# Loading queries by rows of a block and turning them by transposing transfers in half of the batches of a fused attention and Fourier-MLP kernel

## The chip, the core and the metric

The kernel runs on one core of one Trainium2 chip. A core has five engines that run side by side, each with its own queue: PE (TensorE, the matrix unit, whose loads of weights are listed as PEld), DVE (VectorE), ACT (ScalarE), POOL (GpSimd) and SP (SyncE, which here only issues transfers). Transfers issued by SP, ACT or POOL run on 16 DMA engines; those that POOL issues can change the type on the way (here float32 in HBM to float16 in SBUF). The metric is the device time of one execution in microseconds. The profile is one execution, recorded by the hardware profiler.

## The reference

Shapes: four batches, eight heads, 768 tokens in eight blocks of 96, head size 64, model width 512, hidden width 2048.

```python
P = sort_net                                   # (4, 8, 8, 8)
for _ in range(5):                             # softmax of rows, then columns scaled to 1
    P = exp(P - max(P, -1)); P = P / sum(P, -1); P = P / sum(P, -2)
k_sorted = einsum('bhij,bhjcd->bhicd', P, k_b) # blocks of k and v mixed by P
v_sorted = einsum('bhij,bhjcd->bhicd', P, v_b)
scores = q_b @ k_sorted.T / 8                  # within each block of 96 only
attn = softmax(scores)
x = attn @ v_sorted                            # -> (4, 768, 512)

u = x + real(fft(fft(x, axis=1), axis=2))
un = (u - mean(u)) / sqrt(var(u) + 1e-6)
out = u + relu(un @ w_ch1) @ w_ch2
```

## The kernel before

**Stages.** For each batch there are five stages. The mixing makes `kz` (the sorted keys, channels on partitions) and `vs` (the sorted values) by matmuls with `kron`, a spread-out form of the sort matrix. The queries are turned so that channels lie on partitions (`qT`). The attention goes over four pairs of heads `hp`, each in two halves `y` of four blocks. The Fourier stage makes both transforms from folded sums and differences by matmuls with constant cosines and sines. The MLP runs over two groups of three tiles of tokens: 64 matmuls of 384 columns (line 1180), a relu, and 48 matmuls of 512 columns (line 1198), then the output is added and stored. Weights lie in SBUF for the whole run. The main program goes through the batches and hands out the steps of batch b's attention, of batch b+1's loads and mixing, of batch b's Fourier stage and its MLP.

**The order.** Nothing is issued at once. Each piece of work is a step with a name, a batch, the engines that could do it and an assumed duration, the buffers it reads and writes, and, for transfers, an assumed time on the DMA engines (`work`, `hop`). At the end `Plan.run` simulates the engines and puts out one step after the other, the one with the earliest start and among near ones the one with the best priority. Priorities and release times come from tables with an entry for each step's name and batch (`LEAD`), for single steps (`MOVE`) and for loads (`REL`, in nanoseconds). So every engine's queue has a fixed order, written by this planner. `fill` puts dummy matmuls (`unread`, line 687) into planned gaps of PE as long as the plan's clock is below `FILL_END`. Before a load that is marked `bulk=2`, `before` picks an earlier load that has to have landed first, and POOL waits for it with a copy of one element (line 493); POOL's later work queues behind that.

**Buffers** are taken from rings: three each for a pair's keys and queries (`k16`, `q16`), six for its values (`v16`), four for turned queries (`qT`), three for exponentials (`es`, `eT`).

**Loads.** A pair of heads of q, k or v is one transfer by POOL's queue (lines 559 and 569). Partition p takes six tokens that follow each other in HBM, 6p to 6p + 5, so one piece in HBM is 6 x 64 float32 values, 1536 bytes, and a load has 128 x 2 pieces.

**Queries.** `q_mix` turns a pair by 12 transposes on PE through the identity into one bank of PSUM (line 800), and one copy by ACT or DVE writes `qT` (lines 547 and 551). Because of the load, tokens within a block come out as `PERM`: place 16 g + c holds token 6 c + g. That order goes through the attention and is undone by the constants of the Fourier stage and by the selection matrix `rsel`, which are built with `PERM`. In batches 1 to 3 the transposes of a pair are one step with that pair's key matmuls (`psQK`); in batch 0 they are steps of their own (`psQ`).

**Attention.** In batches 0 and 1 (`4 * b + hp < TURN`) `maxima` and `scores` compute the products twice, the second time with keys on partitions, so that the exponentials need no turning. In batches 2 and 3 `turned` computes them once, with queries on partitions; the exponentials are turned by transposing transfers on SP's queue (step `turn_e`, line 912), two for each half. SP's queue also has the transposes of normalised rows (`turn_u`, line 1153, batches 1 to 3) and the moves of sorted values from `vo` to `vs` (line 783).

Of the kernel before, what the change touches and what calls it, by code (L numbers as in the profile page):

```python
# [10 lines left out]
F16 = mybir.dt.float16  # L11
# [6 lines left out]
S = 768  # L18
D = 64
NB = 8  # L20
BLK = 96
KM = BLK + 24
G = 6
# [4 lines left out]
SCALE = 0.125  # L28
TURN = 8
# [5 lines left out]
PERM = np.array([6 * (p % 16) + p // 16 for p in range(BLK)])  # L35
# [172 lines left out]
class Plan:  # L208
# [5 lines left out]
    FILL_LOW, FILL_END, WINDOW = 1931, 49895, 3413  # L214
    LAG, PE_TAIL, MARGIN, NEAR = 45.0, 250.0, 120.0, 14.0
    PORT, PORT_WAIT = ("fold", "fold_d", "minus", "nm", "un", "xem", "kron"), 450.0
    OVER = {"V": 80, "A": 100}
    SPARE = 909
    REL = dict(cdh=38223, cse=17364, cso=12887, idx=43588, load_k2=82421, load_k3=45767, load_q1=32871,
        load_q2=83959, load_q3=155044, load_v1=26759, load_v2=99397, load_v3=18886, rsel=30643, w0=38071,  # L220
        w1=51566, w2=7303, w3=34666, w4=62534, w5=56660, w6=23527, w7=18919)
    LEAD = dict(P=(-10.9, -33.1, 10.8, 47.7), Q=(-21.5, 0, 0, -19.8), We=(-1.6, -0.2, 0.2, 0),
        Wo=(24.9, -10.8, 0, -20.3), a16=(-11.2, -16.6, 1.4, 0), a_out=(26.9, 10.9, 36.1, -20.1),
        add=(-68, 0, 74.6, -10.9), amr=(0.9, 2.6, 18, 0), amt=(-58.6, -2.5, -4.5, 0), const=(15.9, 0, 0, 0),
        exp=(10.9, 48.2, 35.7, -8.7), fold=(-27.1, -23.4, -64.4, 3.7), fold_d=(0, -4.8, 34.7, 0.1),
        hold=(-53, 0, 0, 0), kron=(2.5, 74.7, 2.1, 37.8), kz=(-20.2, 0.8, -52.6, -46.3),
        load_k16=(0, 75.7, 0, -47.8), load_q16=(0, 7.8, -23.1, -0.3), load_v=(0, 26.7, -51.4, -35.5),
        m8=(6.6, 0, 0, 0), max=(-79.4, -48, -32.6, -52.3), minus=(-40.1, -17.1, -9.6, -5.8),
        nm=(-1, -10.8, -13.3, 71.6), norm=(4.5, -39, -29.1, -35.3), ot=(43.5, 40.4, -18.7, 0),
        outt=(0, 0, -51.4, -37), patch=(3.2, 28.2, 5.1, -43.2), pc=(9.3, 0, 0, 0), pca=(19.5, 0, 0, 0),  # L230
        pcol=(-10, 0, 0, 0), pcs=(28.9, 0, 0, 0), ph=(83.6, 26, 3.3, -1.1), psA=(0, 2.4, 0, -26.9),
        psB=(7.1, 0, 2, 26.3), psF=(5.8, -0.3, 0, 19.8), psG=(71.5, 0, 0, 0), psK=(-31.8, 17.3, 37.2, 0.7),
        psM=(-45.2, 0, 0, 0), psN=(-18, -17.6, 7.4, 67), psP=(20.4, 0, 0, 0), psQ=(53.7, -3.6, 23.4, -2.4),
        psQK=(0, 8, 17.6, -16.7), psR=(-1.8, 58.2, 0, 1.6), psRh=(32.2, 16.3, 7.5, -22.1),
        psS=(47.1, 34.2, -65.3, -27.4), psT=(-29.9, -33.5, 0, 0), psV=(-64.4, 0, 24.7, -4.5),
        psWe=(-51.6, 33.5, 1.3, 0), psWo=(4.8, 37.8, 2.9, 0), psX=(26.8, 14.2, -8.8, 0), psY=(0, 25.5, 0, 0),
        psaT=(-0, -2.4, 10.7, 0.2), ptm=(-12.5, 0, 0, 0), qT=(-5.1, 0, 5.8, -57.3), relu=(1.5, 0, 9.6, 81.6),
        root=(0, 9.5, 9.1, -21.3), row_zero=(0, -26.2, -15.6, -2), stats=(-6.4, -23.2, -10.4, 1.7),
        store=(-1.5, 0, -29.6, 6.6), turn_e=(0, 0, 0, -18.6), turn_u=(0, 0, 26.1, 10.7),
        u=(37.5, 8.6, 31.2, -14.6), un=(48.6, 33.2, -20.3, -21.5), unT=(0, 62.4, 0, 15.1),  # L240
        v_move=(-23, 23.6, 0, 26.2), v_sum=(0, -10.6, 0.2, 43), vg=(65.5, 0, 0, 0),
        vo=(14.8, -41.4, -78.1, 0), weights=(62.6, 0, 0, 0), xem=(-20.9, -4.2, 0, -9),
        xom=(-38.7, 63.9, 0, 1.4))
    MOVE = dict(P={(1, 2): 15.5}, add={(2, 2): 0.8, (2, 4): 65.3, (3, 2): 44.7, (3, 4): 9.4},
        amt={(3, 0): -11.9}, const={(0, 3): -19.1},
# [1188 lines left out]
```

## Time and profile before

| | |
|---|---|
| median of 3 runs | 292.35 us (292.27 to 296.48) |
| the profiled execution | 291.53 us, of which 289.7 us lie between its first and last instruction (its span) |
| mean granted clock of PE in it | 0.985 |
| DMA queue q0 (issued by POOL) | 19040 packets, 19.40 MB, 40.6% of 16 engines' span |
| DMA queue q1 (issued by SP) | 31574 packets, 10.28 MB, 18.9% |
| loads of q and of k | 16 each, 192 KB as written |
| transposing transfers | 32 of exponentials, 18 of normalised rows |

A group's row gives the line, the engine, the operation, what it writes and reads, and the count; then the busy time in all and the mean of one in ns; then the idle time of the engine just before such instructions, and what ended it. A row of the timeline gives start and duration in us, the engine, the line and the count, with the idle time before it in brackets. A row of a stretch gives the busy time of each engine in it, with the number of instructions, then the granted clock (1.00 is full), the mean share of the 16 DMA engines' time and GB/s. Matmuls overlap in the array, so the mean of one is its passage and not its share of PE's time; the difference of two starts is.

### The profile page before, as it was taken

The numbers are of one execution on the slowest core, as the hardware profiler recorded it, in microseconds if no ns is written. First come the engines' busy times: TensorE is split into PE (matmuls) and PEld (weight loads), VectorE is DVE, ScalarE is ACT, GpSimd is POOL, SyncE is SP. The second block draws the span as 40 slices with busy tenths as digits, with TensorE's granted clock in tenths as the row PEclk, the third lists the DMA queues.
The fourth block names the chain that finished last, engine by engine and source line by source line (L and its number), as shares of the span: only waits on it lengthen the run. The fifth ranks groups of instructions, "written<-read, shape, count | busy, mean of one in ns | idle before, by whom it ended". The sixth has DMA issues, their size and how long they took to land.

```text
span 289.7 us, 6877 instructions
## 1 busy us (share of the span) xinstructions
PE 276.1 (95%) x2598; PEld 161.9 (56%) x2598; DVE 191.5 (66%) x435; ACT 183.8 (63%) x455; POOL 122.0 (42%) x190
## 2 busy tenths in 40 slices
PE   7899999689999999999999999999999999999993
PEld 2467766257765565445555576455645645645541
DVE  6749988978797897673679998987866572001011
ACT  2368976778894779746495679788725832712700
POOL 8473736314226789765833256230023641112010
PEclk9979999979999999999999999999999999999998
DMA  7998969998856876969935862553311025002002
GB/s 101 182 162 169 154 106 163 185 140 136 107 88 104 112 147 96 124 143 186 130 88 113 154 112 38 115 144 75 70 38 38 36 54 129 36 34 77 1 36 74
DMA packets 50847, 30.41 MB, mean 105 GB/s; under 512 B 25962, under 2 KB 48900, under 8 KB 50812
## 3 DMA queue, kind: packets, MB, share of 16 engines
q0 software_dynamic: 19040, 19.40, 40.6%
q1 hardware_dynamic: 31574, 10.28, 18.9%
q8 instruction: 20, 0.33, 0.5%
q10 hardware_dynamic: 200, 0.30, 0.4%
q14 instruction: 13, 0.11, 0.2%
HBM read 28.50 MB, written 6.29 MB: 120 GB/s over the span
## 4 chain that ended last, share of the span: by engine, by line
PE 78%; DVE 14%; DMA 3%; issue 2%; ACT 1%; DVEq 0%
PE bank L1180 29%; PE bank L1198 24%; PE bank L983 3%; PE bank L853 3%; PE bank L937 3%; DMA eT<-es 2%; PE bank L1088 2%; PE bank L875 2%; PE bank L821 2%; PE bank L761 2%; PE bank L1005 1%; PE bank L800 1%; DVE st L1115 1%; PE bank L1045 1%; DVE mxs L863 1%
## 5 line engine op out<-in xcount | busy, mean ns | idle before, releaser
L1198 PE MATMUL bank<-w2sb,hr 128*128 128x512 f16 x384 | 90.0, 379 | 0.0
L1180 PE MATMUL bank<-unT,w1sb 128*128 128x384 f16 x512 | 89.2, 329 | 0.0
L1186 ACT ACTIVATE hr<-bank 128x384 f16<-128x384 f32 x128 | 60.7, 495 | 38.7 <-PE bank L1180 37.9
L1180 PEld LDWEIGHTS <-w1sb 128*128 128x128 f16 x512 | 49.1, 99 | 32.2 <-issue 1.5
L1219 POOL DMA_INDIRECT out_dram<-outt,idx_sb x22 | 22.6, 1026 | 88.5 <-DVE outt L1207 70.0
L1198 PEld LDWEIGHTS <-hr 128*128 128x128 f16 x384 | 36.0, 98 | 38.2
L1207 DVE SCALAR_TENSOR_TENSOR outt<-u,bank 128x512 f32<-128x512 f32 x24 | 16.4, 682 | 41.8 <-PE bank L1198 41.8
L892 ACT ACTIVATE sm<-bank,mns 96x96 f32<-96x96 f32 x128 | 32.3, 352 | 2.4 <-DVE mns L898 2.0
L944 DVE TENSOR_TENSOR xr<-bank,rz 96x512 f16<-96x512 f32 x32 | 22.0, 686 | 1.1
L547 ACT CAST W<-bank 128x384 f16<-128x384 f32 (+1 forms) x38 | 12.8, 380 | 12.9 <-PE bank L983 8.5
L1115 DVE BATCH_NORM_STATS2 st<-u 128x6 f32<-128x512 f32 x24 | 16.4, 681 | 4.0 <-POOL u L1101 3.9
L863 DVE TENSOR_REDUCE mxs<-bank 96x8 f16<-96x768 f32 x16 | 14.5, 949 | 5.6 <-PE bank L853 5.5
L1100 POOL TENSOR_TENSOR u<-u,PQ 128x257 f32<-128x257 f32 x18 | 12.8, 711 | 9.9 <-DVE PQ L1058 8.6
L898 DVE TENSOR_REDUCE mns<-bank 96x8 f32<-96x768 f32 x16 | 15.0, 944 | 2.6 <-PE bank L853 2.2
L1101 POOL TENSOR_TENSOR u<-u,PQ 128x255 f32<-128x255 f32 x18 | 12.6, 699 | 3.6 <-DVE PQ L1058 3.6
L908 ACT ACTIVATE es<-sm 96x384 f16<-96x384 f32 x19 | 10.0, 528 | 6.1 <-DMA eT<-es 5.8
L880 ACT ACTIVATE sm<-bank 96x768 f32<-96x768 f32 x16 | 12.8, 801 | 1.4 <-PE bank L853 1.2
L922 ACT ACTIVATE eT<-sm 96x768 f16<-96x768 f32 x16 | 13.4, 841 | 0.4
L569 POOL DMA_DIRECT2D k<-in_k_dram x15 | 11.0, 733 | 5.9 <-PE bank L821 4.8
L937 PEld LDWEIGHTS <-eT 97*128 97x128 f16 (+1 forms) x256 | 11.2, 101 | 3.8 <-ACT eT L922 0.5
L943 DVE RECIPROCAL rz<-bank 96x8 f32<-96x8 f32 x32 | 6.3, 197 | 10.6 <-PE bank L937 10.5
L983 PE MATMUL bank<-cso_sb,xso 120*128 120x384 f16 (+1 forms) x64 | 13.1, 326 | 0.0
(144 smaller groups left out, 426.5 us busy)
## 6 DMA issues: line engine op xcount, KB each, us to landing
vs<-vo SPq DMA_DIRECT2D x48, 65.0 KB
v<-in_v_dram POOLq DMA_DIRECT2D x16, 192.0 KB, 4.9
k<-in_k_dram POOLq DMA_DIRECT2D x15, 192.0 KB, 5.5
q<-in_q_dram POOLq DMA_DIRECT2D x15, 192.0 KB, 4.1
w1sb<-in_moe_w_ch_dram POOLq DMA_DIRECT2D x4, 512.0 KB, 8.0
w2sb<-in_moe_w_ch_dram POOLq DMA_DIRECT2D x4, 512.0 KB, 5.9
eT<-es SPq DMA_TRANSPOSE x32
cdh_sb<-cdh SPq DMA_DIRECT2D x1, 387.0 KB
```

The lines of the kernel that those rows point to most:

```text
L863: ("max", b, {"V": 945}, lambda e: nc.vector.tensor_reduce(mxs[n].t.rearrange("p (t j) -> p t j", t=2), pair(pS, BLK), axis=AX.X, op=ALU.max),
L892: nc.scalar.activation(sm.t[:, i], pair(pS, BLK)[:, t, i % 4], AF.Exp, bias=mn.t[:, i:i + 1], scale=-1.0)
L898: ("max", b, {"V": 945}, lambda e: nc.vector.tensor_reduce(mn.t.rearrange("p (t j) -> p t j", t=2), pair(pS, BLK), axis=AX.X, op=ALU.min), ...
L937: nc.tensor.matmul(ps[0:wide(i).stop - BLK * i, i // 4, i % 4], et[0:97, wide(i)], vs[b % 2][:, 4 * y + i % 4, (D + 1) * h:(D + 1) * (h + 1)])
L944: nc.vector.tensor_tensor(xr2[b % 2][0:BLK, 4 * y:4 * y + 4, 128 * hp:128 * hp + 128].rearrange("p j (t d) -> p t j d", t=2), ps[:, :, :, ...
L983: nc.tensor.matmul(ps, x[0:n, j], cso[0:n, j, :], start=(j == 0), stop=(j == 3))
L1115: nc.vector.bn_stats(st.t, us[b, i, m].t)
L1180: nc.tensor.matmul(ps, w1sb[:, mc, 128 * fc:128 * fc + 128], unT[b, gr].t[:, mc, :], start=(mc == 0), stop=(mc == 3))
L1186: nc.scalar.activation(dst, bank(pH, [128, 384]), AF.Relu)
L1198: nc.tensor.matmul(ps, hr[f4].t[:, fc % 4, 128 * t:128 * (t + 1)], w2sb[:, fc, :], start=(fc == 0), stop=(fc == 15))
L1207: step("outt", b, {"V": 687}, lambda e, u=u, pC=pC, o=o: nc.vector.scalar_tensor_tensor(o.t, u.t, RSC, bank(pC, [128, DM]), op0=ALU.mult, ...
L1219: step("store", b, {"G": 1050}, lambda e: nc.gpsimd.indirect_dma_start(out=out.rearrange("b s m -> (b s) m"), out_offset=bass.IndirectOffs ...
```

## The change

- All loads of q get a partition for each row in natural order. In batches 0 and 1, partition p takes tokens 128 g + p for g = 0 to 5 (one transfer, pieces of 64 values, 256 bytes). In batches 2 and 3, partition r of 96 takes row r of each of the eight blocks, in two transfers, one for each head of the pair.
- `PERM` becomes the identity; the copies that write `qT` in batches 0 and 1 become contiguous.
- In batches 2 and 3 the transposes on PE and the copy go. A new step `turn_q`, two for each pair, turns four blocks at a time by a transposing transfer on SP's queue, from `q16` straight into `qT`. The key matmuls of these batches are steps of their own (`psK`).
- A `q16` buffer is 128 x 1024 float16 values in place of 128 x 768; `v16` has five buffers in place of six.
- `TURN` counts batches in place of pairs; which batches use `turned` stays as it was.
- The planner's tables are new throughout, as are some of its settings: `FILL_LOW` 1931 to 1834, `FILL_END` 49895 to 81377, `NEAR` 14 to 68, `SPARE` 909 to 1392, and the release times, among them `load_q1` 32871 to 17265, `load_q2` 83959 to 49545, `load_v3` 18886 to 94052.

```diff
-TURN = 8
+QT = 2
+TURN = 2
...
-PERM = np.array([6 * (p % 16) + p // 16 for p in range(BLK)])
+PERM = np.arange(BLK)
...
-    ring("q16", 3, [128, 2, G * D], F16)
-    ring("v16", 6, [128, 2, G, D], F16)
+    ring("q16", 3, [128, NB, 128], F16)
+    ring("v16", 5, [128, 2, G, D], F16)
...
+    def flat(t, x, by_row):
+        if by_row:
+            return rows(t).rearrange("p h (g d) -> p (h g) d", d=D), x.rearrange("h (g p) d -> p (h g) d", g=G)
+        return t, x.rearrange("h (p g) d -> p h (g d)", g=G)
...
+            if b >= QT and tag == "q16":
+                step("load_q16", b, {"G": 1700}, lambda e, t=d[b, hp]: [nc.gpsimd.dma_start(
+                    t.t[0:BLK, :, D * hh:D * hh + D],
+                    q[b, hs.start + hh].rearrange("(i r) d -> r i d", r=BLK)) for hh in range(2)],
+                    w=[d[b, hp]], work=3000, hop=1750, lanes=2, bulk=2 if b > 1 else 1, need=need, rel=f"load_q{b}")
+                continue
...
-                t.t, src[b, hs].rearrange("h (p g) d -> p h (g d)", g=G)),
-                w=[d[b, hp]], work=1250, hop=1750, bulk=2 if b > 1 else 1, need=need, rel=f"load_{tag[0]}{b}")
+                *flat(t.t, src[b, hs], src is q)),
+                w=[d[b, hp]], work=1250 if tag == "k16" else 1700, hop=1750, bulk=2 if b > 1 else 1, need=need, rel=f"load_{tag[0]}{b}")
...
-            copy(e, qT[b, hp].t.rearrange("x (i g c) -> x i g c", g=G, c=16),
-                 bank(pQ, [128, G, 128], F16).rearrange("x g (i c) -> x i g c", c=16))
+            copy(e, qT[b, hp].t, bank(pQ, [128, S], F16))
+        if b >= QT:
+            for t in range(2):
+                step("turn_q", b, {"S": 1300}, lambda e, t=t: nc.sync.dma_start(
+                    qT[b, hp].t[:, 384 * t:384 * t + 384].rearrange("x (i r) -> x i r", r=BLK),
+                    q16[b, hp].t[0:BLK, 4 * t:4 * t + 4].rearrange("q i x -> q (i x)"), transpose=True),
+                    r=[q16[b, hp]], w=[(qT[b, hp], t)], work=800, hop=900)
+            return
...
+        if b >= QT:
+            q_mix(b, hp)
         mixed = ("kz", b, {"A": 790, "V": 950}, ev, [pK], [("kz", hp)])
-        if b == 0:
+        if b == 0 or b >= QT:
             plan.chain(("psK", b, {"T": 350}, f, [k16[b, hp], (kron[b], hp)], [pK]), mixed)
             return
```

More of the change, by code (lines that the diff above doesn't have):

```diff
@@ L222 @@
[L222 to L243, printed above, removed]
@@ L244 @@
[L244 to L253 removed]
+    SPARE = 1392
@@ L562, in load_v, with rows @@
             w=[v16[b, hp]], work=1200, hop=1800, bulk=2 if b > 1 else 1, need=need, rel=f"load_v{b}")
+    def flat(t, x, by_row):
+        if by_row:
+            return rows(t).rearrange("p h (g d) -> p (h g) d", d=D), x.rearrange("h (g p) d -> p (h g) d", g=G)
+        return t, x.rearrange("h (p g) d -> p h (g d)", g=G)
+    def rows(t):
+        return t if t.shape[1] == 2 else t.rearrange("p i x -> p (i x)")[:, 0:2 * G * D].rearrange(
+            "p (h x) -> p h x", h=2)
     def load_kq(b, hp, need, q_first=False):
```

80 lines of the change are left out of this document (59 added, 21 removed).

## The prediction, written before the changed kernel was run

> **What bounds the kernel now.** I read the head of the page first, then the chain that ended last, then a table of stages that I cut where the work changes: at 12.3 us the softmax iterations on the sort matrix end, at 60.5 us the first matmul of batch 0's MLP starts, at 221.8 us only the last of batch 2's MLP is left beside the end of batch 3's attention, and at 243.7 us batch 3's own MLP starts.
>
> ```profile
> span 289.7 us, 6877 instructions
> PE 276.1 (95%) x2598; PEld 161.9 (56%) x2598; DVE 191.5 (66%) x435; ACT 183.8 (63%) x455; POOL 122.0 (42%) x190
> ...
> PE 78%; DVE 14%; DMA 3%; issue 2%; ACT 1%; DVEq 0%
> ```
>
> ```profile
> 12.30:60.50 48.20, 42.72 (x627) 28.95 (x627) 39.77 (x92) 36.44 (x66) 24.95 (x35) 0.95 0.96 154
> 60.50:100.00 39.50, 39.50 (x500) 25.45 (x499) 31.21 (x67) 30.42 (x65) 15.35 (x28) 0.97 0.77 116
> 100.00:160.00 60.00, 58.98 (x512) 33.73 (x511) 43.90 (x89) 42.07 (x123) 39.22 (x67) 1.00 0.81 129
> 160.00:221.80 61.80, 61.74 (x554) 35.41 (x553) 51.45 (x112) 44.85 (x136) 17.11 (x24) 1.00 0.43 91
> 221.80:243.70 21.90, 21.90 (x134) 12.11 (x133) 12.00 (x28) 10.69 (x26) 11.23 (x15) 1.00 0.22 55
> 243.70:285.30 41.60, 41.51 (x224) 21.73 (x222) 4.13 (x6) 15.57 (x32) 4.84 (x5) 1.00 0.16 48
> ```
>
> In each row stand the stretch, its length, the busy time of PE, PEld, DVE, ACT and POOL, the granted clock, the DMA share and GB/s. There are two regimes. Up to 60.5 us PE leaves 5.48 us of 48.2 idle, DVE is busy for 39.8 us and the DMA engines are taken for 96% of the time: this stage is set by DVE and by transfers. From 60.5 to 285.3 us PE is idle for 0.00 + 1.02 + 0.06 + 0.00 + 0.09 = 1.2 us in all, at a clock of 0.97 to 1.00. There the MLP of one batch fills PE under the attention of the next, so what leaves PE's queue shortens the run one for one, as long as the other engines keep up.
>
> **The transposes that leave PE.** For batches 2 and 3 each of the eight pairs of heads loses 12 transposes through the identity (line 800). Two pairs of the last batch and one of batch 2 in PE's timeline, with the group's row:
>
> ```profile
> 116.49 0.53 PE L800 MATMUL bank<-ident,q 128*64 128x128 f16 x12
> 116.85 0.50 PE L821 MATMUL bank<-kron,k 128*64 128x128 f16 x12
> ...
> 167.12 0.53 PE L800 MATMUL bank<-ident,q 128*64 128x128 f16 x12
> 167.47 0.50 PE L821 MATMUL bank<-kron,k 128*64 128x128 f16 x12
> 168.04 0.53 PE L800 MATMUL bank<-ident,q 128*64 128x128 f16 x12
> 168.37 0.53 PE L821 MATMUL bank<-kron,k 128*64 128x128 f16 x12
> ```
>
> ```profile
> L800 PE MATMUL bank<-ident,q 128*64 128x128 f16 x180 | 8.1, 228 | 0.5 <-DMA q<-in_q_dram 0.4
> ```
>
> The 228 ns of one is its passage and overlaps with its neighbours. What counts is from start to start of the next group: 0.36, 0.35 and 0.33 us. I take 0.35 us, and 8 x 0.35 = **2.8 us** leave the queue in the stretch where PE is full. The k matmuls behind them stay, so no turn between array shapes is saved. The Trainium skill ("TensorE: Matmul & The Clock Gate", "Part 4: PE-mode transpose") has about 275 ns for one such transpose in a kernel; 96 of them would then be an estimated 26 us, and the trace, with 12 in 0.35 us, does not agree.
>
> **The evictions that leave with them.** Between 84 and 200 us the queries were moved out of PSUM like this:
>
> ```profile
> L551 DVE COPY qT<-bank x6: 540/543/558, 93.5 to 181.3; 128x768 f16<-128x768 f16 x6
> L547 ACT COPY qT<-bank x2: 793/822/852, 117.4 to 168.7; 128x768 f16<-128x768 f16 x2
> ```
>
> That frees 6 x 0.54 = 3.3 us of DVE and 2 x 0.82 = 1.6 us of ACT. I cost it at nothing: in those stages the end is PE's, and DVE has 16 of 60 and 10 of 61.8 us to spare. At the most it takes away part of PE's 1.2 us of waits. In batches 0 and 1 the copies stay, only their target becomes contiguous; their rows are those of a copy of 768 elements and I leave them as they are.
>
> **The order and the fill.** All lead times of the planner change, and dummy matmuls may now go into PE's gaps up to 81.4 us instead of 49.9. Between 50 and 60 us PE idles, and the first MLP matmuls behind that run slowly:
>
> ```profile
> 50.00:60.00 10.00, 6.13 (x59) 3.69 (x58) 9.61 (x29) 7.02 (x16) 4.04 (x7) 0.96 1.06 161
> ```
>
> ```profile
> 60.49 2.47 PE L1180 MATMUL bank<-unT,w1sb 128*128 128x384 f16 x8
> 62.80 0.61 PE L1162 MATMUL bank<-ident,un 128*128 128x128 f16 x8
> ...
> 67.67 1.47 PE L1180 MATMUL bank<-unT,w1sb 128*128 128x384 f16 x8
> 68.98 0.51 PE L875 MATMUL bank<-small_sb,mxs 96*128 96x96 f16 x8
> ```
>
> The same eight matmuls take 2.31 us to the next start at 60.5 and 1.31 us at 67.7. Dummies in the gap can win back at most that 1.0 us; they win nothing if planned idle and real idle do not meet. A dummy that meets work delays it by a fraction of a microsecond. I take the middle, **0.5 us**. What the other lead times do, no row can say; it is in the rivals.
>
> **The loads of q.** All 16 now read pieces of 256 B: 128 x 12 (batches 0 and 1) or 2 x 96 x 8 (batches 2 and 3), 1536 pieces in either form, where there were 256 of 1536 B. The trace has no such load. Nearest rows, by stretches in which one kind of packet prevails: from 2 to 12 us (loads of 1536 B), 48 to 58 us (with weight rows of 2 KB), 129 to 140 us (mostly moves of v, 520 B) and 193 to 209 us (transposing transfers, 256 B).
>
> ```profile
> q0 software_dynamic: 1926, 1.40, 105.0%
> ```
>
> ```profile
> q0 software_dynamic: 1897, 1.71, 115.3%
> ```
>
> ```profile
> q1 hardware_dynamic: 1630, 0.74, 29.7%
> ```
>
> ```profile
> q1 hardware_dynamic: 4672, 1.11, 34.9%
> ```
>
> The share times 16 engines times the stretch, over the packets, gives 87, 97, 32 and 19.1 ns for one. So a load takes 256 x 87 / 16 = 1.4 us of all engines today. At 19.1 ns the new one takes 1536 x 19.1 / 16 = 1.8 us, 0.44 us more; at 87 ns it would take 8.4, 7.0 us more. I take 19.1 ns, since the piece is of that size and one engine's time for a packet should grow with its bytes; both ends stay for the range. A gain is excluded, as the bytes are the same. The eight loads of batches 0 and 1 then cost 3.5 us of DMA time ahead of the weights. What covers it:
>
> ```profile
> 40.78 0.72 POOL L569 DMA_DIRECT2D q<-in_q_dram x1 [4.35 <-PE bank L800]
> ...
> 82.81 0.29 POOL L493 COPY landed<-w2sb 1x1 f16<-1x1 f16 x1 [7.51 <-DMA w2sb<-in_moe_w_ch_dram]
> ```
>
> ```profile
> 63.99 0.53 PE L800 MATMUL bank<-ident,q 128*64 128x128 f16 x12
> ...
> 88.61 1.03 PE L1198 MATMUL bank<-w2sb,hr 128*128 128x512 f16 x4
> ```
>
> Batch 1's last query load is issued at 40.8 us, and the first of that batch's queries are turned only at 64.0. The last part of w2 has landed at 82.8 and is first used at 88.6: 5.8 us of cover, more than 3.5. So this costs **0** at 19.1 ns, and the excess over 5.8 us beyond it. Batch 2 and 3 loads have 19% and 57% of the DMA time free (stages above). The Trainium skill ("DMA: Bandwidth & Descriptors", "Specifications") wants at least 512 B for full rate and says that smaller pieces are written by read-modify-write, which speaks against this load; no row here shows it for a load.
>
> **POOL and the buffer of v.** Eight loads are issued in two halves, and each issue writes more pieces:
>
> ```profile
> L569 POOL DMA_DIRECT2D q<-in_q_dram x15 | 11.0, 732 | 5.0 <-PE bank L800 4.3 <-issue 0.5
> L1236 POOL DMA_DIRECT2D w2sb<-in_moe_w_ch_dram x4 | 3.1, 771 | 0.5 <-issue 0.5
> ```
>
> From 256 to 512 pieces an issue grows by about 40 ns, so 768 pieces should take some 0.8 us: 8 more issues are about 6 us of POOL, plus the waits of later loads for earlier ones to land. Behind them queue the sums of v, the additions to u and the stores; POOL is idle for 21 us between 100 and 160 and for 45 us of the next stage, and I cost it at nothing. Without that cover each half would delay an addition by 0.8 us. One v buffer fewer holds a load back until one more reader is done:
>
> ```profile
> 137.44 0.74 POOL L559 DMA_DIRECT2D v<-in_v_dram x1 [0.88 <-PE bank L1180]
> ```
>
> Such a wait exists, of 0.9 us, and is hidden. Zero again.
>
> **SP's queue.** Sixteen transposing transfers are added, of the shape of those that turn the exponentials.
>
> ```profile
> L912 SPq DMA_TRANSPOSE eT<-es x32: 1180/1200/2384, 98.3 to 208.3; - x32
> ```
>
> ```profile
> 177.16 3.16 SPq L1153 DMA_TRANSPOSE unT<-un x2
> ...
> 192.99 16.50 SPq L912 DMA_TRANSPOSE eT<-es x11
> ```
>
> ```profile
> 238.81 0.81 ACT L1138 ACTIVATE un<-u,nm,rstd 128x512 f16<-128x512 f32 x1 [2.44 <-DMA unT<-un]
> ...
> 243.52 2.76 PE L1180 MATMUL bank<-unT,w1sb 128*128 128x384 f16 x16
> ```
>
> At 1.2 us each they are 9.6 us of SP for a batch. Behind them on SP stand the turns of the exponentials, the moves of v and the turns of the normalised rows, and PE's values and MLP wait for those. From 177.2 to 209.5 us SP's queue is full; a turn of q put in there pushes all that by 1.2 us. The end of that chain is batch 3's third normalised tile: its transfer has landed by 238.8, when its buffer is taken again, and PE starts that MLP at 243.5. So there are 4.7 us of slack, of which a run shorter by 3.3 us uses most. If the turns of q come before 177 us the cost is 0, which I take.
>
> **The sum.** The profiled execution took 291.53 us, 1.8 more than its span. 291.5 - 2.8 - 0.5 = 288.2. The median of the runs shown, 292.35, lies 0.8 above that execution, so the forecast for a median is **289.0 us**, 1.1% less.
>
> **Rivals.** *The pieces of q choke the early DMA.* At 32 ns a load costs 1536 x 32 / 16 - 1.4 = 1.7 us more, eight cost 13.4, and 13.4 - 5.8 = 7.6 us show: 289.0 + 7.6 = 296.6. Between 87 and 97 ns lie 512 B, so a line through these two puts 256 B at some 62 ns: 8 x (5.95 - 1.4) - 5.8 = 30.6, about 320 us. It decides from 22 ns on, where eight loads use up the 5.8 us. For it speaks that only the rows of q0 are reads from HBM with a cast; against it, that packets there overlap (105%) and so look longer than they are, and that batch 0's MLP is not the only work PE has. This is also the way in which the 512 B rule of the Trainium skill's DMA page would act. Chance 0.20; half of it above 298.
> *SP's queue takes the gain.* Four turns of q within the full stretch push the chain by 4.8 us; with the slack of 4.7 and PE earlier by 3.3, 3.4 us show, and the time is 289.0 + 3.4 = 292.4, no change. For it speaks that the last query copy of batch 3 started at 181.3 us, inside that stretch; against, that batch 2's last queries leave their buffer at 116.9 us, so that batch 3's can be loaded and turned long before 177 us. Chance 0.15.
> *The new order also empties the early stage.* PE's 5.5 us of idle before 60.5 us and the clock behind it are worth up to 6.5 us; half of it, instead of my 0.5, gives 286.2, all of it 283.0. For it: every lead time there is new. Against: DVE, at 39.8 of 48.2 us, loses no work there. Chance 0.25.
> *The forecast itself*: 0.40.
>
> **Chances and range.** Two per cent, about what a measurement of this kernel can tell from no change, is 5.8 us: below 286.5 or above 298.2. Faster: four fifths of the third rival and little else, 0.21. Slower: half of the first rival, 0.10, and 0.01 for mishaps. Within: 0.68. The range runs from 284.5, the middle of the third rival, to 296.5, the first rival at 32 ns.
>
> **What would show it.** In the new profile line 800 has 96 matmuls fewer, PE is still full from about 60 us on, and the last MLP starts some 3 us earlier. Query loads that land in more than about 6 us, or PE waiting for w2 or k before 90 us, mean the first rival; a PE gap before the last MLP, with SP full ahead of it, the second; PE idle before 60 us well under 5.5 us, the third. If PE idles by more than 3 us after 60 us, the step that what leaves PE leaves the run was wrong.

## The result and the profile after

| | before | after |
|---|---|---|
| median | 293.26 us (292.27 to 296.48, 4 runs) | 302.41 us (300.36 to 302.99, 4 runs) |
| ratio of the times, 95% interval | 1 | 1.0355 [1.0304, 1.0406] |
| profiled execution, span | 291.53 us, 289.7 us | 302.81 us, 299.8 us |
| first MLP matmul, last one with `w1sb`, begin at | 60.5 us, 274.5 us | 66.5 us, 284.6 us |

A ratio counts only executions within 1.5% of the fastest of their kernel, so it is not the quotient of these medians. The change makes the kernel slower by 3.0 to 4.1%. The forecast was 289.0 us, 1.1% faster, with a range that ended at 296.5. The head of the page of the changed kernel, its queue of POOL's transfers, and the chain that ended last:

```profile
span 299.8 us, 6731 instructions
PE 278.2 (93%) x2513; PEld 159.2 (53%) x2513; DVE 188.5 (63%) x430; ACT 183.7 (61%) x452; POOL 133.4 (45%) x198
...
q0 software_dynamic: 39648, 19.40, 47.2%
...
PE 64%; DVE 16%; DMA 9%; ACT 4%; issue 3%; POOL 2%; SPq 0%; DVEq 0%; POOLq 0%; ACTq 0%
```

PE has 85 matmuls fewer and is busy for 2.1 us more; its idle time grew from 13.6 us (289.7 - 276.1) to 21.6. Its share of the chain fell from 78% to 64%, and DMA, ACT and POOL came in. The same stages as before (columns as there), of the changed kernel:

```profile
12.30:60.50 48.20, 40.76 (x623) 27.75 (x623) 38.78 (x82) 32.51 (x57) 28.05 (x37) 1.00 1.21 166
60.50:100.00 39.50, 37.15 (x476) 23.41 (x475) 30.55 (x70) 31.31 (x61) 12.13 (x21) 1.00 0.74 97
100.00:160.00 60.00, 58.29 (x479) 31.70 (x472) 39.20 (x78) 38.02 (x114) 44.47 (x73) 1.00 0.80 132
160.00:221.80 61.80, 58.19 (x468) 32.53 (x467) 48.82 (x111) 46.15 (x143) 21.56 (x30) 1.00 0.66 108
221.80:243.70 21.90, 21.90 (x161) 13.01 (x160) 13.38 (x31) 14.13 (x34) 8.81 (x13) 1.00 0.11 38
243.70:285.30 41.60, 41.60 (x226) 22.01 (x225) 7.34 (x15) 17.56 (x39) 7.08 (x8) 1.00 0.20 57
```

Idle time of PE is the length of a stretch less its busy time. Before 60.5 us it rose from 5.48 to 7.44 us. From 60.5 to 285.3 us it rose from 1.2 to 2.35 + 1.71 + 3.61 = 7.7 us. So the regime in which PE is full is gone. The clock is 1.00 throughout, where before it was 0.95 to 1.00, so it explains nothing of the loss.

The edit itself is there. Groups of the changed kernel by line, with the transposes of queries that are left and the dummies, and the issue groups of its query loads (line 600 for batches 0 and 1, line 595 for 2 and 3) and of the turns (ns min/median/max):

```profile
L831 PE MATMUL bank<-ident,q 128*64 128x128 f16 x84 | 3.7, 221 | 0.8 <-DMA q<-in_q_dram 0.5 <-DVE u L1140 0.2
...
L718 PE MATMUL bank<-junk 128*128 128x512 f16 x19 | 5.4, 379 | 0.3 <-DVE u L1140 0.3
```

```profile
L595 POOL DMA_DIRECT2D q<-in_q_dram x16: 769/778/853, 87.7 to 181.5; - x16
...
L600 POOL DMA_DIRECT2D q<-in_q_dram x7: 1017/1035/1099, 2.5 to 30.5; - x7
```

```profile
L838 SPq DMA_TRANSPOSE qT<-q x16: 1179/1248/1971, 92.0 to 196.0; - x16
```

The 180 transposes are 84; there are 19 dummies of line 718 where there were 8, 2.8 us more of them; a turn takes 1.2 us of SP, as was said. The first MLP matmul is 6.0 us late and the last one 10.1, so over half of the loss is made before the MLP begins.

### The profile page after: what moved, and what is told of

Read it like the earlier page. It is cut to its first block, busy times and chain, and to the rows that moved or that the text cites. A ratio compares the mean times of both kernels' runs of the same rounds, so it can differ in the third digit from the quotient of the medians.

```text
span 299.8 us, 6731 instructions
## 1 busy us (share of the span) xinstructions
PE 278.2 (93%) x2513; PEld 159.2 (53%) x2513; DVE 188.5 (63%) x430; ACT 183.7 (61%) x452; POOL 133.4 (45%) x198
## 4 chain that ended last, share of the span: by engine, by line
PE 64%; DVE 16%; DMA 9%; ACT 4%; issue 3%; POOL 2%; SPq 0%; DVEq 0%; POOLq 0%; ACTq 0%
PE bank L1219 24%; PE bank L1237 21%; DMA eT<-es 3%; DVE xr L983 3%; PE bank L892 2%; DVE vo L803 2%; DMA unT<-un 2%; PE bank L1127 2%; DMA q<-in_q_dram 2%; PE bank L1022 2%; DVE st L1154 2%; PE bank L914 1%; PE bank L858 1%; PE bank L1084 1%; PE bank L976 1%
## 5 line engine op out<-in xcount | busy, mean ns | idle before, releaser
L1237 PE MATMUL bank<-w2sb,hr 128*128 128x512 f16 x384 | 87.7, 379 | 0.0
L1219 PEld LDWEIGHTS <-w1sb 128*128 128x128 f16 x512 | 48.3, 98 | 34.2 <-DMA unT<-un 2.2
L1237 PEld LDWEIGHTS <-hr 128*128 128x128 f16 x384 | 36.6, 98 | 40.5
L563 ACT CAST W<-bank 128x384 f16<-128x384 f32 (+1 forms) x41 | 13.6, 381 | 13.9 <-PE bank L1022 7.2
L1177 ACT ACTIVATE un<-u,nm,rstd 128x512 f16<-128x512 f32 x12 | 9.4, 809 | 12.9 <-DMA unT<-un 10.3
L976 PE MATMUL bank<-vs,eT 97*128 97x65 f16 (+1 forms) x256 | 12.8, 196 | 1.3 <-issue 0.6
L595 POOL DMA_DIRECT2D q<-in_q_dram x16 | 12.5, 787 | 2.1 <-issue 1.3
L575 POOL DMA_DIRECT2D v<-in_v_dram x16 | 12.3, 773 | 0.8 <-issue 0.3
L1127 PE MATMUL bank<-xr,rsel_sb 97*128 97x512 f16 (+3 forms) x48 | 11.6, 384 | 1.0 <-DMA xr<-xr 0.6
```

The source lines that it names most:

```text
L976: nc.tensor.matmul(ps[0:wide(i).stop - BLK * i, i // 4, i % 4], et[0:97, wide(i)], vs[b % 2][:, 4 * y + i % 4, (D + 1) * h:(D + 1) * (h + 1)])
L1127: nc.tensor.matmul(ps[p0:p0 + w], rsel[0:n, m, c0:c0 + w], xr[0:n, 7 - j if m else j, :], start=(y == 0 or i == 1), stop=(y == 1 or i == 1 ...
L1219: nc.tensor.matmul(ps, w1sb[:, mc, 128 * fc:128 * fc + 128], unT[b, gr].t[:, mc, :], start=(mc == 0), stop=(mc == 3))
L1237: nc.tensor.matmul(ps, hr[f4].t[:, fc % 4, 128 * t:128 * (t + 1)], w2sb[:, fc, :], start=(fc == 0), stop=(fc == 15))
```

## The experiments

The milestones in this table are the begin of the first and of the last matmul with `w1sb`, in each run's profile (that of run l is of an execution of 295.64 us, which its ratio does not count). Where there is a time and no ratio, it is one execution.

| run | what it is | ratio to before | first, last (us) |
|---|---|---|---|
| a | order of before, q in 256-byte pieces | 1.0077 [1.0007, 1.0147] | 59.0, 274.8 |
| e | order of before, no turning of q in batches 2 and 3 | 0.9891 [0.9821, 0.9961] | 60.7, 273.8 |
| l | order of before, loads of the change, no turning | 1.0026 [0.9984, 1.0068] | 60.6, 278.7 |
| f | order of before, loads and turns of the change | 1.0221 [1.0113, 1.0328] | 58.8, 282.4 |
| p | f for batch 3 alone | 1.0134 [1.0024, 1.0244] | 59.6, 278.2 |
| r | f, turns read landed data | 1.0177 [1.0112, 1.0243] | 61.0, 280.2 |
| o | f, turns issued by ACT | 1.0707 [1.0571, 1.0844] | 60.8, 292.3 |
| c | kernel before, tables of the change | 1.0441 [1.0352, 1.0529] | 67.5, 287.1 |
| b | changed kernel, tables of before | 1.0926 [1.0850, 1.1003] | 60.3, 299.4 |
| g | changed kernel, tables of before for batches 0 and 1 | 1.1142 [1.1063, 1.1222] | 61.7, 310.9 |
| d | changed order, q in 1536-byte pieces | 1.0328 [1.0258, 1.0397] | 67.0, 284.1 |
| h | changed order, no turns on SP | 1.0290 [1.0202, 1.0377] | 66.3, 282.2 |
| i | changed order, 96 transposes back on PE | 1.0374 [1.0268, 1.0479] | 65.5, 284.3 |
| j | changed order, batch 1's sums of v left out | 1.0287 [1.0173, 1.0400] | 64.7, 283.1 |
| k, m, n, q | changed kernel, some release times of before | 326.75, 311.10, 313.65, 316.35 us | below |

### One part at a time

**Run a**: the kernel before with the new pieces; what was one long row for each partition is twelve short ones.

```diff
-PERM = np.array([6 * (p % 16) + p // 16 for p in range(BLK)])
+PERM = np.arange(BLK)
...
-                t.t, src[b, hs].rearrange("h (p g) d -> p h (g d)", g=G)),
+                *((t.t.rearrange("p h (g d) -> p (h g) d", d=D), src[b, hs].rearrange("h (g p) d -> p (h g) d", g=G))
+                  if src is q else (t.t, src[b, hs].rearrange("h (p g) d -> p h (g d)", g=G)))),
```

> The kernel before, with every engine's order of instructions kept, but all 16 loads of q in pieces of 256 B (and the natural order of queries). Theory 1 (the small pieces crowd the early DMA queue): the first MLP matmul comes some 5 us later than at 60.5 us and the time is 298 to 300 us. Theory 2 (the new order of steps costs the time) and theory 3 (the transposing transfers on SP's queue cost it): no change, 292 to 294.5 us.

**Run d**: the changed order with long pieces; three memsets fill the part of `q16` that then is not loaded. Queries come to wrong places.

```diff
-            return rows(t).rearrange("p h (g d) -> p (h g) d", d=D), x.rearrange("h (g p) d -> p (h g) d", g=G)
+            return rows(t), x.rearrange("h (p g) d -> p h (g d)", g=G)
...
-                    t.t[0:BLK, :, D * hh:D * hh + D],
-                    q[b, hs.start + hh].rearrange("(i r) d -> r i d", r=BLK)) for hh in range(2)],
+                    rows(t.t)[:, hh], q[b, hs.start + hh].rearrange("(p g) d -> p (g d)", g=G)) for hh in range(2)],
```

> The changed kernel, with every engine's order kept (three small memsets are added at the start), but all loads of q in pieces of 1536 B; queries then stand in the wrong places of their blocks, and for batches 2 and 3 the wrong halves of the buffers are turned. Theory 1: the time falls by 5 us or more, to 297 us or below. Theories 2 and 3: 301 to 303 us as with the small pieces.

The pieces cost 0.8% in the order of before, and in the new order d cannot be told from the changed kernel (1.0328 against 1.0355, intervals overlap). The queue's total in run a:

```profile
q0 software_dynamic: 39520, 19.40, 49.3%
```

Before, 19040 packets took 0.406 x 16 x 289.7 = 1882 us of engine time. Here 39520 take 0.493 x 16 x 290.0 = 2288. The 20480 added packets cost 406 us, 19.8 ns each. A load of 1536 pieces thus takes 256 x 87 + 1280 x 19.8 = 47.6 us of engine time, 31 ns for a piece and 1.6 us of all engines more than before: the first rival's lower price. Yet of the 25 us for 16 loads the kernel shows 2.2. For the same bytes the engines work about twice as long (47.6 against 22.3 us). That agrees in direction with the Trainium skill ("DMA: Bandwidth & Descriptors", "Specifications"), which asks for at least 512 B for full rate. The price in time was small; which work covered the rest, no run tells.

**Run e**: nothing but the transposes and copies of batches 2 and 3 is left out, so those queries are stale.

```diff
         fq, rq, wq, turn = q_mix(b, hp)
+        if b >= 2:
+            fq, turn = (lambda e: None), turn[:3] + (lambda e: None,) + turn[4:]
```

> The kernel before, order kept, with the 96 transposes and 8 copies that turn the queries of batches 2 and 3 left out (those batches are scored with queries of batches 0 and 1 that still lie in the buffers). It prices the first term of the prediction's sum alone. If what leaves PE leaves the run, 2.5 to 3.5 us less than before (ratio 0.988 to 0.991). If batch 3's attention, and not PE's queue, sets when the last MLP starts, less than 1 us (ratio over 0.996).

The ratio gives a gain of 1.1% [0.4, 1.8], 3.2 us, where 2.8 had been worked out. But it counts the three shortest of run e's ten executions (287.1 to 290.8 us). The mean of all ten is 292.4 us at a mean granted clock of 0.983; the thirteen executions of the kernel before that go with them have the same mean at the same clock. The head of run e's page:

```profile
span 289.0 us, 6671 instructions
PE 274.2 (95%) x2502; PEld 159.4 (55%) x2502; DVE 189.7 (66%) x429; ACT 181.9 (63%) x453; POOL 122.7 (42%) x190
```

PE is busy for 1.9 us less than before and idle for 1.2 us more, which leaves 0.7 us. So it is not shown that the kernel before shortens by what leaves PE. **Run i** asks the same of the changed kernel, by putting as many transposes back (of keys, into a bank that the key matmuls overwrite):

```diff
+        def back(e):
+            if b >= QT:
+                q4 = k16[b, hp].t.rearrange("p h (g d) -> p h g d", d=D)
...
+                        nc.tensor.matmul(ps[64 * hh:64 * hh + 64, g, :], q4[:, hh, g, :], ident, is_transpose=True)
+            f(e)
```

> The changed kernel in its own order, with 96 transposes put back on PE: 12 (of the pair's keys, into the bank that the key matmuls overwrite) ahead of the key matmuls of each pair of batches 2 and 3; their results are not used. If what stands in PE's queue from 60 us on lengthens the run one for one, as the prediction had it, the time is 2.8 us above the changed kernel's: about 305 us, ratio to the kernel before 1.045. If PE's idle time in the changed kernel (15 us in all up to 222 us, after waits for others) takes them up, it stays within 1 us: ratio 1.035 to 1.039.

```profile
L873 PE MATMUL bank<-ident,k 128*64 128x128 f16 x96 | 4.2, 222 | 0.3 <-DVE xr L991 0.3
```

The 96 are in run i's groups, and the ratio is 1.0374 against 1.0355. The middles do not differ by the 2.8 us, and the profile agrees (span 299.6 us against 299.8), as if PE's idle time took them up; the interval takes in the other expectation, 1.045, as well.

### The order

**Run c** gives the kernel before the new tables and settings and nothing else; **run b** gives the changed kernel the old ones.

> The kernel before with the planner's tables and settings of the changed one. Theory 2: 298 to 304 us, with the first MLP matmul at 64 us or later. Theories 1 and 3: within 3 us of 293 us.

> The changed kernel with the planner's tables and settings of the kernel before. Theory 1: still 299 to 303 us, since pieces and transfers are the same. Theory 2: most of the loss goes, 290 to 295 us. Theory 3: 297 us or more, with PE gaps after 100 us as in the changed kernel. The planner still works out a new order from other assumed durations, so a few us either way are its own.

Both lose, c 4.4% without any other edit, and b 9.3%. Tables are made for one set of steps, and here each meets the steps of the other kernel, so neither number is the price of the order within the changed kernel. What they share with other runs is the first milestone: 65.5 to 67.5 us wherever the early part is planned by the new tables (after, c, d, h, i), 58.8 to 61.7 us with the old ones (before, a, b, e, f, g). So the 6 us before the MLP come from the order, not from the loads or the turns. With the old tables the changed kernel loses later; the wait list of run b:

```profile
PE bank L1204 <- DMA unT<-un: 15.1, 2, 11.2
```

Around the longer of these two waits the granted clock falls as well:

```profile
160.00:222.00 62.00, 46.36 (x377) 26.01 (x376) 41.57 (x89) 39.80 (x129) 29.01 (x45) 0.83 0.66 98
```

So part of such a loss is PE running slower: the profiled execution of b has a mean clock of 0.947 and that of g 0.932, where the kernel before has 0.985.

**Run g** was to take the best of both: old tables for batches 0 and 1, new ones behind.

> The changed kernel with the lead times of before for batches 0 and 1, its settings and its early release times, and the new lead times for batches 2 and 3. If the loss lies in the order of the first two batches (6 us by the first MLP matmul), that matmul comes at 59 to 61 us and the time is 294 to 297 us (ratio 1.005 to 1.02). If it needs the late part as well, the first MLP matmul is early and the time stays at 300 us or more.

Its first MLP matmul came at 61.7 us as expected, and its time, 326 us, was far off: two waits for the same kind of transfer take 21.0 us.

**Run j** takes one thing out of the early part. In the changed kernel's timeline of DVE and of POOL:

```profile
31.22 1.65 DVE L999 TENSOR_TENSOR xse<-xr 96x512 f16<-96x512 f16 x1
32.79 0.67 DVE L999 TENSOR_TENSOR xso<-xr 96x512 f16<-96x512 f16 x1
33.38 0.94 DVE L902 TENSOR_REDUCE mxs<-bank 96x8 f16<-96x768 f32 x1
```

```profile
31.64 0.93 POOL L612 TENSOR_TENSOR vh<-v 128x384 f32<-128x384 f16 x1
```

A fold that takes 0.42 us elsewhere takes 1.65 while POOL adds parts of v. Batch 0's eight folds by line, from 30 to 47 us, in the changed kernel, then in run j:

```profile
L999 DVE TENSOR_TENSOR xse<-xr 96x512 f16<-96x512 f16 x4 | 3.2, 816 | 0.1
L999 DVE TENSOR_TENSOR xso<-xr 96x512 f16<-96x512 f16 x4 | 2.8, 728 | 0.0
```

```profile
L1001 DVE TENSOR_TENSOR xse<-xr 96x512 f16<-96x512 f16 x4 | 1.6, 418 | 0.1
L1001 DVE TENSOR_TENSOR xso<-xr 96x512 f16<-96x512 f16 x4 | 1.6, 416 | 0.0
```

```diff
         def f(e):
+            if b == 1:
+                return
             v4 = v16[b, hp].t
```

> The changed kernel in its own order, with the twelve POOL sums of v of batch 1 (31.6 to about 50 us) left out; its sums are those of batch 0. Theory: in the new order batch 0's eight folds run on DVE at the same time as these sums, take 6.0 us in place of 3.4, and the first MLP matmul is late by that: it comes at about 64 us in place of 66.5, and the time falls to about 300 us (ratio 1.026). Rival: the folds are not what ends last before the first MLP matmul; it stays at 66 to 67 us and the ratio at 1.03 to 1.04.

Without the sums the folds take 3.2 us in place of 6.0, and the MLP begins at 64.7 us, 1.8 earlier, about a third of the early loss. The ratio falls to 1.0287, with intervals that overlap. That the folds make this third is not shown, since run j also frees POOL: in run d the same folds take 4.9 us (2.8 + 2.1) and the MLP begins at 67.0 us, in run c 4.3 (2.7 + 1.6) and 67.5.

**Runs k, m, n and q** plan the changed kernel with some of the release times (`REL`) of before and all new lead times: k all those of constants, weights and batch 1's loads; m the constants alone; n batch 1's loads alone; q constants and weights. The three parts are:

```diff
-cdh=9230, cse=25964, cso=13805, idx=53957, rsel=8646
+cdh=38223, cse=17364, cso=12887, idx=43588, rsel=30643
...
-w0=24262, w1=36772, w2=50670, w3=43365, w4=31852, w5=29416, w6=6897, w7=55598
+w0=38071, w1=51566, w2=7303, w3=34666, w4=62534, w5=56660, w6=23527, w7=18919
...
-load_k1=12849, load_q1=17265, load_v1=15890
+load_q1=32871, load_v1=26759
```

The constants, in SP's queue before and after:

```profile
16.86 0.32 SPq L1243 DMA_DIRECT2D cse_sb<-cse  x1
```

```profile
25.68 1.01 SPq L1282 DMA_DIRECT2D cse_sb<-cse  x1
```

> The changed kernel, planned with the release times of the kernel before for the constants, the weights and batch 1's loads; all lead times stay new. If the early loss comes from when loads and constants are issued (cosines at 25.7 us, where the kernel before had 16.9; batch 1's queries at 17.2), the first MLP matmul comes at 60 to 62 us in place of 66.5. If it comes from the order in which the engines take the work (the lead times), it stays at 65 to 68 us. On the time of the whole no theory has a figure, since the plan of the later stages moves with it: 295 to 310 us.

> The changed kernel, planned with the release times of before for the constants alone (cosines, sines, selection matrix, indices). If the late constants (cosines issued at 25.7 us in place of 16.9) hold batch 0's Fourier stage, the first MLP matmul comes at 60 to 62 us in place of 66.5. If it is batch 1's early loads of queries and what they let DVE do early, it stays at 65 to 67 us.

> The changed kernel, planned with the release times of before for batch 1's loads of queries, keys and values alone. If batch 1's work, which the early loads let DVE and POOL take ahead of batch 0's folds and norms, is the cause, the first MLP matmul comes at 59 to 62 us in place of 66.5. If the constants are the cause, it stays at 65 to 67 us.

> The changed kernel, planned with the release times of before for the constants and the eight parts of the weights; batch 1's loads of q, k and v keep the new ones. If the weights' place among POOL's loads makes up what the constants alone left, the first MLP matmul comes at 58 to 61 us, as with all release times put back (58.6). If it takes batch 1's late loads as well, it stays at 63 to 65.

The first MLP matmul came at 59.8 us in k, 64.0 in m, 67.7 in n and 63.4 in q (the 58.6 of the last expectation is where k begins to load the weights for it). With all of them put back the early loss is gone, though every lead time is new: it hangs on release times. No part does it alone: the constants give 2.5 us of the 6.7, the weights 0.6 more, batch 1's loads nothing by themselves and the rest only together with the others. Each of these is a new plan and one execution. All four lose more behind and end 9 to 24 us above the changed kernel; in k's list of waits:

```profile
PE bank L1172 <- DMA unT<-un: 19.9, 2, 11.3
```

What makes those rows late, when the early part is faster, these runs do not settle.

### The turns on SP's queue

**Run f** has the change's loads and turns in the order of before: each turn is put into SP's queue as soon as its load has landed by the plan. For space, two small buffers share others, and `v16` keeps six.

```diff
+        for t in range(2):
+            nc.sync.dma_start(x.t[:, 384 * t:384 * t + 384].rearrange("x (i r) -> x i r", r=BLK),
+                              q16[b, hp].t[0:BLK, 4 * t:4 * t + 4].rearrange("q i x -> q (i x)"), transpose=True)
+
+    def hook(at):
+        for b, hp in sorted(turns):
+            if b > 1 and turns[b, hp].fin is not None and at >= turns[b, hp].land:
+                turn_q(b, hp)
...
-            fq(e)
+            if b < 2:
+                fq(e)
```

> The kernel before with the loads by rows and the transposing transfers of the change, but every engine's other instructions in the order of before; the two turns of a pair stand in SP's queue where the planner's clock has the load landed. The change without its new tables. The order is the cause (theory 2): within 3 us of before, ratio 0.99 to 1.01. The transfers on SP's queue are (theory 3): 298 us or more, ratio over 1.02, with PE waiting for the turned exponentials or for kz and qT after 90 us.

**Run l** is f without the 16 turns (the loop with `nc.sync.dma_start` above goes); its queries of batches 2 and 3 are stale.

> The kernel of run f (the order of before; loads of q in 256-byte pieces, two halves for batches 2 and 3) without its 16 transposing transfers of q: the queries of batches 2 and 3 are stale and PE does not wait for them. If the transfers, with the landing that they wait for, are what cost f its 2.2%, the ratio is that of run e with the price of the pieces, 0.989 + 0.008 = about 0.997. If POOL's 8 further issues and the pieces cost it, it stays at about 1.02.

So the loads without any turning are at 1.0026. The ratios of e and a would add up to 0.9968, with an interval of 0.7% to either side of each, so a price of the eight further issues cannot be told from zero. The turns make the rest of run f, 2.0%. Where PE waits in run f between 88 and 200 us, and what SP has queued:

```profile
94.29 0.42 PE L890 MATMUL bank<-kz,qT 64*128 64x96 f16 x6 [2.07 <-DMA qT<-q]
96.33 0.58 PE L890 MATMUL bank<-kz,qT 64*128 64x96 f16 x10 [1.62 <-DMA qT<-q]
...
194.73 0.43 PE L974 MATMUL bank<-vs,eT 97*128 97x65 f16 x8 [2.38 <-DMA eT<-es]
```

```profile
176.15 3.28 SPq L817 DMA_DIRECT2D vs<-vo  x4
179.55 5.77 SPq L578 DMA_TRANSPOSE qT<-q  x4
185.42 2.52 SPq L1190 DMA_TRANSPOSE unT<-un  x2
188.04 3.80 SPq L949 DMA_TRANSPOSE eT<-es  x3
```

There are two prices: at 94 us PE waits for the turned queries themselves, and at 194.7 for exponentials whose turn stood behind four turns of q and two of normalised rows. Before, the first of those two began at 177.2 us; here at 185.4. Behind its waits PE also runs at a lower granted clock in run f, 0.86 and 0.91 in these stretches, where before it was 1.00:

```profile
80.00:100.00 20.00, 16.31 (x130) 9.04 (x128) 12.36 (x29) 9.79 (x26) 13.36 (x23) 0.86 1.07 110
...
140.00:160.00 20.00, 17.59 (x153) 9.76 (x152) 11.96 (x29) 11.53 (x35) 8.01 (x13) 0.91 0.66 85
```

**Run r** separates them: the same 16 transfers at the same places, read from weights that landed long before.

```diff
-                              q16[b, hp].t[0:BLK, 4 * t:4 * t + 4].rearrange("q i x -> q (i x)"), transpose=True)
+                              w2sb[0:BLK, 0, :], transpose=True)
```

> The kernel of run f, with its 16 transposing transfers at the same places of SP's queue and of the same shape, but read from the weights of the second MLP matrix, landed long before: nothing in SP's queue waits for a load of q. The queries of batches 2 and 3 are not the reference's. If the wait for the load, which holds all that stands behind on SP, is what cost f its 2 per cent over the loads alone (1.0026), the ratio falls to 1.00 to 1.01. If the 1.2 us of SP and the traffic of each transfer cost it, it stays at 1.015 to 1.025.

```profile
95.13 0.39 PE L890 MATMUL bank<-kz,qT 64*128 64x96 f16 x10 [0.53 <-DMA qT<-w2sb]
```

```profile
190.98 0.43 PE L974 MATMUL bank<-vs,eT 97*128 97x65 f16 x8 [2.98 <-DMA unT<-un]
```

Of 3.7 us at 94 us, 0.5 are left, and PE is busy for 2.8 us less than in run f with the same 2502 matmuls (273.9 against 276.7 us, at a mean clock of 0.987 against 0.974); the gap ahead of batch 3's first values stays, 3.0 us. The ratio, 1.0177, lies 0.4% under f's with intervals that overlap, and 1.5% over l's with intervals that do not: most of the price is the place in SP's queue and the traffic, not the landing of the load.

**Run p** leaves batch 2 as before and uses the turns for batch 3 alone (against run f):

```diff
-            if b > 1 and src is q:
+            if b == 3 and src is q:
...
-            if b < 2:
+            if not (b == 3):
```

> The kernel of run f with batch 2 as before (loaded with keys' pieces of tokens in 256-byte form, turned on PE) and the transposing transfers for batch 3 alone. PE's waits at 94 and 96 us (3.7 us in 80 to 100) go. If half of f's loss comes from each batch, the ratio is about 1.01. If batch 3's turns, in SP's full stretch, make all of it, it stays at 1.02; if batch 2's waits made it, it falls to 1.00 or, with the transposes of batch 3 saved, to 0.995.

At 1.0134 somewhat over half of f's loss is there with one batch, though the interval reaches from 1.0024 to 1.0244. In it is the wait before batch 3's first values, 2.0 us at 188.9, behind eight turns and six moves of v on SP from 164.5 to 179.8 us.

**Run o** issues the same turns from ACT's queue:

```diff
-            nc.sync.dma_start(x.t[:, 384 * t:384 * t + 384].rearrange("x (i r) -> x i r", r=BLK),
+            nc.scalar.dma_start(x.t[:, 384 * t:384 * t + 384].rearrange("x (i r) -> x i r", r=BLK),
```

> The kernel of run f, with its 16 transposing transfers of q issued by ACT in place of SP. If f lost its 2.2% because the turns of exponentials, of normalised rows and the moves of v queue behind them on SP, the ratio falls to that of run l and a little more for ACT's time, 1.00 to 1.01, and the first PE wait for turned queries at 94 us stays. If ACT is held as long as SP was (1.2 us each, and its wait for the load in front), exponentials and evictions come late and the ratio is 1.03 or more. If only the wait for the loads' landing counts, it stays at 1.02.

```profile
91.51 3.74 ACTq L578 DMA_TRANSPOSE qT<-q  x2
95.34 0.59 ACT L549 COPY u<-bank 128x512 f32<-128x512 f32 x1 [3.95 <-issue]
```

A turn takes as long to issue there, and ACT's evictions stand behind it: 7% slower.

**Run h** takes the turns out of the changed kernel.

```diff
-                step("turn_q", b, {"S": 1300}, lambda e, t=t: nc.sync.dma_start(
-                    qT[b, hp].t[:, 384 * t:384 * t + 384].rearrange("x (i r) -> x i r", r=BLK),
-                    q16[b, hp].t[0:BLK, 4 * t:4 * t + 4].rearrange("q i x -> q (i x)"), transpose=True),
+                step("turn_q", b, {"S": 1300}, lambda e: None,
```

> The changed kernel, order kept, without the 16 transposing transfers of queries (batches 2 and 3 are scored with queries of batches 0 and 1). Theory 3: the time falls by 5 us or more, to 297 us or below. Theory 2: it falls by less than 2 us, since SP's queue and the loads behind it were not what PE waited for.

There they cost 0.65% by the middles of the ratios (1.0355 to 1.0290), less than the intervals' width. SP's queue of the changed kernel between 177 and 198 us, and PE's longest wait behind it:

```profile
177.26 1.21 SPq L838 DMA_TRANSPOSE qT<-q  x1
...
183.03 2.63 SPq L838 DMA_TRANSPOSE qT<-q  x2
185.71 0.59 SPq L814 DMA_DIRECT2D vs<-vo  x1
186.40 2.50 SPq L951 DMA_TRANSPOSE eT<-es  x2
188.96 1.25 SPq L838 DMA_TRANSPOSE qT<-q  x1
190.30 3.06 SPq L1192 DMA_TRANSPOSE unT<-un  x2
193.46 1.20 SPq L951 DMA_TRANSPOSE eT<-es  x1
194.77 2.50 SPq L838 DMA_TRANSPOSE qT<-q  x2
```

```profile
200.20 4.72 PE L1219 MATMUL bank<-unT,w1sb 128*128 128x384 f16 x28 [1.70 <-DMA unT<-un]
```

In the new order turns of q stand between the others, and with the new tables the kernel loses 3.6%, where the old ones make it 9.3%. The new order pays for that with the early part. No variant of the change beat the kernel before. Run l has the loads of the change and no turning at all, neither on PE nor on SP, and is at 1.0026: in the old order even turns at no cost would have won 0.2% at the most.

## Why the prediction was wrong

**The order** is the step that failed first. The prediction wrote "What the other lead times do, no row can say", took 0.5 us of gain for the fill and nothing for the rest, and its rival for the order could only gain more. An unknown cost that no row bounds has two sides. Here the order loses: the MLP begins 6.0 us late in the changed kernel, and the new tables alone cost the kernel before 4.4% (run c). The sentence "DVE, at 39.8 of 48.2 us, loses no work there" looked at the wrong thing: DVE lost no work, but its folds took 6.0 us where run j has 3.2, and the constants came 8.8 us later; with the release times of before for constants, weights and loads the 6 us were gone (run k). Release times had moved by up to 75 us (`load_v3`; `load_q1` by 15.6, `cse` by 8.6) and were not followed to their transfers and to what these let DVE begin.

**"What leaves PE's queue shortens the run one for one, as long as the other engines keep up"** is the term of -2.8 us, and the runs do not establish it. In the order of before run e's ratio has it, its ten executions together and its profile (0.7 us) do not. In the changed order the condition fails: by the prediction's own test PE might idle for 3 us after 60 us, and it idles for 7.7. Run i fits that, within an interval that is wider than the term.

**SP's queue** was costed at 0 on a condition, "If the turns of q come before 177 us". Six of the eight turns of batch 3 begin later, at 177.3 to 196.0 us, so the condition of the second rival held; it was given 0.15. Its mechanism is the one that run f shows, a chain through SP that ends in a gap of PE. Its price there, 2.0% or 5.8 us for 16 turns, is above the 3.4 us worked out: run f also shows PE waiting for the first turned queries of batch 2, and a lower clock behind its waits. In the changed order the price is about 2 us, not told from zero.

**The pieces of q**, costed at 0, are worth 0.8% [0.1, 1.5] in the old order. A piece takes 31 ns and not 19.1, which is near what an *added* one costs (19.8). That is the first rival's lower row, but its 7.6 us did not show: it had taken the wait for w2 as the only cover. Which other work covered the rest, no run tells.

**POOL, the evictions, the buffer of v.** The issue with 768 pieces took 0.78 us, as reckoned, and the one of 1536 took 1.03. Run l, with pieces and further issues and without transposes, is at +0.3%, so these terms are small; what the issues cost beside the pieces is within the intervals. The evictions and the buffer of v were not tried by themselves.

The sum, in the order of before: the loads of the change without any turning make +0.3% (run l) and the turns add 2.0, which is the +2.2% of run f. The change with its own order adds 1.3% to that, with intervals that overlap a little. So even with nothing reordered the forecast gain of 1.1% is not there, and SP's queue makes it a loss; the new order then moved the loss to the front rather than removing it. What stays open is which of the release times must move together, whether the 2.8 us of PE show in any order, and PE's busy time, which rose by 2.1 us: the added dummies only make up for the transposes.

## What to carry to other kernels

A kernel whose PE is full has an order that was fitted to its queues; an edit that moves work to a queue which already has a full stretch is costed by what stands behind it there, and the order that comes with the edit is a term with both signs, to be bounded by the first milestone of each stage. To see which it is, run the edit in the old order and the new order without the edit: two runs that split the loss before any theory. A saving reckoned at a full engine can be lost where that engine has gaps, and one of 1% has to show in all executions, not in the shortest alone.

## What the runs showed of the hardware

- **Elementwise work of POOL stretches that of DVE.** A fold of two inputs in SBUF took 1.65 us in place of 0.42 while POOL added values, and 0.42 again without it (run j). The Trainium skill ("SBUF — State Buffer", "Who interferes with whom") says that a DVE instruction with two SBUF inputs contends with a GpSimd instruction that reads SBUF. The trace agrees, with 2.8 us over eight folds; the fold shown began 0.42 us ahead of POOL's addition and was stretched all the same.
- **Packets of a transfer overlap**, so that a stretch's share goes over 100%; the difference of two queue totals (406 us for 20480 packets) gave the price of a piece that no single stretch did.
- **A transposing transfer takes 1.2 us of the issuing engine** on ACT as on SP (1277 and 1233 ns in the middle), and an engine that computes loses that time.
- **Behind long waits PE got a lower clock.** The granted clock was 0.83 from 160 to 222 us in run b, around a wait of 11.2 us, and 0.86 from 80 to 100 us in run f, behind waits of 2.1 and 1.6 us; in the changed kernel, whose longest wait after 60 us is 1.7 us, it was 1.00. Not each wait of 2 us does it: run c has one of 2.1 us at 177.6 us, and its clock stays at 1.00 there.
